# Three tiles of x loaded one by one ahead of the second weights, in a matmul with 2:4-pruned weights

## The chip, the cores and the metric

The kernel runs on one core of a Trainium2 chip. The metric is the device time of one execution in microseconds (us), the median of several runs. A profiled execution gives the trace: when every instruction of every engine started and ended, when every transfer was issued and when it landed.

TensorE (PE) multiplies, and loads its stationary operand beside that (PEld). VectorE (DVE), ScalarE (ACT) and GpSimd (POOL) work elementwise. SyncE (SP) and ScalarE issue the transfers (DMAs).

## The reference

```
x: (16, 512, 1024) bf16    w: (1024, 1024) bf16    b: (1024) bf16

wg   = w.reshape(256, 4, 1024)            # groups of 4 rows, for each column
mag  = abs(wg)
thr  = the second largest of each group's 4 magnitudes
mask = (mag >= thr)
wp   = (wg * mask).reshape(1024, 1024)
out  = einsum("bsd,df->bsf", x, wp) + b
```

So of every four weights that follow each other along the input dimension, the two largest in magnitude stay; the product is that of 8192 tokens with the pruned weights.

## The kernel before

**Tiles.** The 8192 tokens are 64 tiles of 128. The input dimension (1024) is cut into two halves of 512 (g = 0 and 1), the output dimension into halves or quarters. A tile's full product is 16 matmuls of 128x128 by 128x512: 8 steps along the input for each of two output halves.

**The weights and their pieces.** The first half of the weights (g = 0) comes in four pieces of 256 columns (pieces 0 to 3), the second (g = 1) in two of 512 (pieces 4 and 5). Each is loaded with the four members of a group side by side (`w_sb`, `load_w`), so that VectorE can compare them elementwise: abs; `hi` and `lo`, the larger and the smaller of each pair; `t1`, the smaller of the two `hi`; `t2`, the larger of the two `lo`; `thr`, the larger of `t1` and `t2`; `mask`; `mult`, which writes the pruned weights `wp` (class `Piece`, L155 to L193; L177 is abs, L166 the others). Piece 0's four loads are split by rows between two queues (L124, L125); the loads of piece 1 (L130) are called "the second weights" here.

**The start.** TensorE can use `wp` at once only against x in the same order, with the four members of a group apart. For the first seven tiles (`NPK`) this is made on TensorE: a tile's first 512 inputs are loaded as they lie (`load_x`), transposed by four matmuls against a unit matrix (`transpose`, L197 to L203, into a PSUM buffer of the pool `psum_t`, two buffers, or, for tile 4, of `psum_o`, six buffers) and copied out by ScalarE (`copy_xt`, L207). Then each of these tiles is multiplied with pieces 0 to 3 as soon as they are pruned (`mm_piece`, L236). Two tiles share a PSUM bank (`pairs`), and ScalarE copies a finished bank to SBUF (`stage`, L272).

**After that** all tiles use weights in natural order: `spread` (L153) copies `wp` to `wp_nat` by DMA, and x comes transposed by DMA (`load_lead` L118, `load_low` L244, `load_nat` L416). Matmuls against `wp_nat` are at L250. `closes` finishes the first twelve tiles, a loop goes over the other 52. VectorE adds the bias on the way out (L442, L444), ScalarE's queue stores. The last `LATE` tiles are stored in two halves each, the others in one store.

**The orders.** While the weights are pruned, the order on each engine is written out as a list of tokens (L274 to L296), one list for each engine. A planner, not part of the kernel, made them; `run` (L399) only emits each engine's tokens in that order, once what a token needs has been emitted. The tokens are these:

- `T5a` transposes tile 5, `C5a` copies it out, `F4` is four filler matmuls.
- `M5.0g` multiplies tile 5 with part g of piece 0. Parts: x and y are the first and the last two members of the groups; u, v, one member each; g and h the last two members, columns 0 to 127 and 128 to 255 of the piece.
- `abs1`, `hi1`, ..., `mult1x` are the pruning steps of piece 1; `S3b0` stages a pair's bank, `U6h0` tile 6's.
- `W0.1` spreads weights, `X1` and `Y1` are loads of transposed x, `Z` loads the last weights and the bias, `E0`, `A0h0` start products against `wp_nat`.

An instruction waits where it stands in its engine's list, and all that is behind it waits too. TensorE starts with 20 fillers (L409, L410), which read constants only.

The loads at the start are issued in this order, on SP's queue unless "act" is named:

```
    load_w(0, 0, 256, 0, 2)
    load_w(0, 0, 256, 2, 4, "act")
    load_x(5, 6, "act")
    load_x(SOLO, SOLO + 1, "act")
```

(`SOLO` is tile 6), and then L129 to L136: tiles 3 and 4 in one transfer, the second weights, tile 2, tiles 0 and 1, the weights of pieces 2, 3 and 4, and the transposed load of tiles 7 to 11.

Of the kernel before, what the change touches and what calls it, by code (L numbers as in the profile page):

```python
# [10 lines left out]
def kernel(  # L11
# [8 lines left out]
    P = 128  # L20
    bf16 = mybir.dt.bfloat16
    fp32 = mybir.dt.float32
# [10 lines left out]
    FH = 512  # L33
# [8 lines left out]
    STG = 8  # L42
    SOLO = 6
    GROUPS = ((0, 3), (3, 6), (6, 7))
    LATE = 6
    sizes = (4, 8, 8, 8, 8, 8, 8)
    batches = []
    t0 = NPK + LEAD
# [11 lines left out]
    psum_t = ctx.enter_context(tc.tile_pool(name="psum_t", bufs=2, space=bass.MemoryType.PSUM))  # L60
    psum_o = ctx.enter_context(tc.tile_pool(name="psum_o", bufs=6, space=bass.MemoryType.PSUM))
# [38 lines left out]
    def issue(eng, out_, in_):  # L100
        q = nc.sync if eng == "sp" else nc.scalar
        return seq(eng, q.dma_start(out_, in_))  # L102
# [4 lines left out]
    def load_x(ta, tb, eng="sp"):  # L107
        xs = const.tile([P, tb - ta, HK], bf16, name=f"x_{ta}")
        xv, n = tokens(xf, ta)
        issue(eng, xs[:], xv[:, n:n + tb - ta, :HK])  # L110
        for t in range(ta, tb):
            x_sb[t] = xs[:, t - ta, :]
# [13 lines left out]
    load_x(5, 6, "act")  # L126
    load_x(SOLO, SOLO + 1, "act")
    act(nc.scalar.activation(spark[:], nc.const_aps.tensor(1.0, [P, 1], bf16), Act.Abs))
    load_x(3, 5)  # L129
    load_w(0, 256, 512)  # L130
    load_x(2, 3)
    load_x(0, 2)
    load_w(0, 512, 768)
    load_w(0, 768, 1024)
# [58 lines left out]
                self.tt(wp[:, self.g, ms, self.c0 + ca:self.c0 + cb], self.w[:, ms, ca:cb], self.mag[:, ms, ca:cb], Alu.mult)  # L193

    xpk = {}

    def transpose(t):  # L197
        xg = x_sb[t].rearrange("p (q m) -> p m q", m=4)
        bank = psum_o.tile([P, FH], fp32, name="ps") if t == 4 else psum_t.tile([P, FH], fp32, name="tp")
        tp = bank[:].bitcast(bf16)[:, :FH].rearrange("p (m q) -> p m q", m=4)  # L200
        for m in range(4):
            pe(nc.tensor.transpose(tp[:, m, :], xg[:, m, :], ident[:]))  # L202
        xpk[t] = tp  # L203
# [4 lines left out]
        xpk[t] = xt  # L208

    ps_open = {}  # L210
    SPLIT = {0: 6}
    part = {"": slice(0, 4), "x": slice(0, 2), "y": slice(2, 4), "a": slice(0, 2), "b": slice(2, 4)}
    part.update({c: slice(m, m + 1) for m, c in enumerate("uvst")})
    part.update({c: slice(2, 4) for c in "gh"})
    cols = {"g": (0, 128), "h": (128, 256), "j": (0, 128), "k": (128, 256)}
    half = {"a": slice(0, 1), "b": slice(1, 2)}
    pairs = [(3, 4), (SOLO, NPK), (0, 1), (2, 5)]
    pair_of = {t: q for q, pr in enumerate(pairs) for t in pr}
# [48 lines left out]
    def stage(key):  # L267
        solo = key[1] == "h"
        q, h, at = (pair_of[key[0]], key[2], int(key[0] != SOLO)) if solo else (key[0], key[1] // 2, key[1] % 2)
        if (q, h) not in staged:  # L270
# [2 lines left out]

    order = {  # L274
# [7 lines left out]
        ),  # L282
        "dve": (
# [4 lines left out]
        ),  # L288
        "act": (
            "C5a C3a C4a C6a C2a C0a C1a S3b0 S2b0 abs3 S0b0 U6h0 S3b1 S0b1 S2b1 S3b2 S0b2 S2b2 S2b3 S0b3 U6h1 "  # L290
            "S3b3 U7h0 W1.0q U7h1"
        ),
        "sp": (
            "W0.0 Z W0.1 X1 W1.0p Y1 W1.1 Y0"
# [1 line left out]
    }  # L296
    written = {"X0"}
    p = {}
    halves = {0: tuple("ghuv"), 1: ('x', 'y'), 2: ('u', 'v', 'y'), 3: ('x', 'y')}

    by_rows = {0}

# [1 line left out]
        return [tok + x for x in halves.get(i, ("",))]  # L304

    def split_tok(tok):
        k = tok[-1] if tok[-1] in "xyabuvstghjk" else ""
        return (tok[:-1] if k else tok), k

    transposed = []  # L310

    def needs(eng, tok):
        base, k = split_tok(tok)
        if tok[0] == "C":
            return ["T" + tok[1:]]
        if tok[0] == "T":
            return ["C" + transposed[-2]] if tok != "T4a" and len(transposed) > 1 else []
        if tok[0] == "F":
            return []
        if tok[0] == "W":  # L320
            g, h = map(int, tok[1:4].split("."))
            return [n for i, pc in enumerate(pieces) if pc[0] == g and pc[1] // FH == h for n in all_of(f"mult{i}", i)]
        if tok[0] in "XYZ":
            return ["A0h1"] if tok == "Y1" else []
        if tok[0] == "A":
            return ["X0", f"W0.{tok.split('h')[1]}"] + ([f"U{NPK}h{tok[-1]}"] if tok[1] == "3" else [])
        if tok[0] == "E":
            return ["X0", f"W0.{tok[1]}"]
        if tok[0] == "U":
            t, h = map(int, tok[1:].split("h"))  # L330
            if t == NPK:
                return [f"E{h}"]
            return [f"M{t}.{x}" for i, pc in enumerate(pieces) if pc[0] == 0 and pc[1] // FH == h for x in all_of(str(i), i)]
        if base[0] == "M":
            t, i = base[1:].split(".")
            return [f"C{t}a", f"mult{i}{k}"]
        if tok[0] == "S":
            q, n = map(int, tok[1:].split("b"))
            return [f"M{t}.{x}" for i, pc in enumerate(pieces) if pc[0] == 0 and pc[1] // CW == n
                    for t in pairs[q] for x in all_of(str(i), i)]  # L340
        i, step = base[-1], base[:-1]
        before = {"abs": [], "hi": ["abs"], "lo": ["abs"], "t1": ["hi"], "t2": ["lo"],
                  "thr": ["t1", "t2"], "mask": ["thr", "hi", "lo"], "mult": ["mask"]}[step]
        out_ = []
        for b_ in before:
            if b_ in ("t1", "thr") and int(i) in SPLIT:
                out_ += [b_ + i + s for s in {"j": "j", "k": "k", "g": "j", "h": "k"}.get(k, "jk")]
            elif b_ == "t2":
                out_.append(b_ + i)
            elif b_ in ("abs", "hi", "lo") and int(i) in by_rows:  # L350
                out_ += [b_ + i + k] if step in ("hi", "lo") else [b_ + i + s for s in "ab"]
            else:
                out_.append(b_ + i + (k if b_ == "mask" else ""))
        return out_

    def emit(eng, tok):
        base, k = split_tok(tok)
        if tok[0] == "T":
            transpose(int(tok[1:-1]))
            if tok != "T4a":  # L360
                transposed.append(tok[1:])
        elif tok[0] == "F":
            filler(int(tok[1:]))
        elif tok[0] == "W":
            g, h = map(int, tok[1:4].split("."))
            spread(g, h * FH, (h + 1) * FH, {"": range(4), "p": range(2), "q": range(2, 4)}[tok[4:]], eng)
        elif tok[0] == "Z":
            load_w(1, 512, 1024)
            sp(nc.sync.dma_start(bias_sb[:], b.partition_broadcast(P)))
        elif tok[0] == "X":  # L370
            xnat.update(load_lead(int(tok[1:])))
        elif tok[0] == "Y":
            xnat.update(load_low(int(tok[1:])))
            if tok == "Y1":
                tc.add_manual_dep(tails["sp"].ins, ends["A0h1"].ins.name, SYNC, reason="let the spread of the lower weights pass")
        elif tok[0] == "E":
            open_solo(int(tok[1:]))
        elif tok[0] == "U":
            t, h = map(int, tok[1:].split("h"))
            stage((t, "h", h))  # L380
        elif tok[0] == "A":
            open_nat(*map(int, tok[1:].split("h")))
            ends[tok] = tails["pe"]
        elif tok[0] == "C":
            copy_xt(int(tok[1:-1]))
        elif tok[0] == "M":
            mm_piece(*map(int, base[1:].split(".")), part[k], cols.get(k))
        elif tok[0] == "S":
            stage(tuple(map(int, tok[1:].split("b"))))
        else:  # L390
            i = int(base[-1])
            if i not in p:
                p[i] = Piece(i)
            if eng == "act":
                p[i].abs_act()
            else:
                p[i].do(base[:-1], part.get(k, slice(0, 4)), half.get(k, slice(0, 2)), cols.get(k))
# [82 lines left out]
    for bi, (tb, nb) in enumerate(batches):  # L480
        if bi:
            load_batch(bi + 1)
        for j in range(nb):
            t = tb + j
            xt = xnat[t]
            o = outp.tile([P, Dout], bf16, name="o")
            if t == NT - 1:
                for n, (c0, c1) in enumerate(((0, FH), (FH, FH + CW), (FH + CW, Dout - P), (Dout - P, Dout))):
                    ps = psum_o.tile([P, FH], fp32, name="ps")
# [44 lines left out]
```

## Time and profile before

| | |
|---|---|
| Median of 3 runs | 232.64 us (232.62 to 232.73) |
| The profiled execution | 232.79 us |
| Its span, first instruction to last | 231.0 us |
| VectorE busy | 107.8 us, 47% |
| ScalarE busy | 13.3 us, 6% |
| Matmuls against `wp_nat` (L250, x from `xb`) | 831, 178.9 us busy, 375 ns each |
| Products of the first seven tiles (L236) | 126, 12.9 us busy, 261 ns each |
| Transposes (L202, into `tp`) | 24, 2.1 us busy, 220 ns each |
| Transfers, mean over the span | 165 GB/s |

The profile counts an engine as busy from an instruction's start to its modelled end. Matmuls are pipelined: one starts well before the one in front of it has ended, so the distance from start to start is what an instruction costs, and the mean time of one is longer. The chain of work that ended last is followed back from the last instruction: at each step to what released it, or to the instruction before it on its engine. In rows in order of time the first number is the start, the second the length, both in us, and x is the count; "L250" is a line of the kernel. "Idle before" is an engine's idle time and what ended it. For a transfer the last number is the time from issue to landing.

### The profile page before, as it was taken

To read this page: it belongs to the slowest core of one execution; us is meant where nothing else is said; L and a number is where in the kernel's file an instruction comes from. 1 tells how busy PE (TensorE), PEld (TensorE's weight loads), DVE (VectorE), ACT (ScalarE), POOL (GpSimd) and SP (SyncE) were. 2 spreads that over 40 slices of the span, in tenths; PEclk is the share of its full clock that TensorE was granted. 3 is DMA by queue.
4 is the path that set the end of the run, shared out by engine and by line. 5 is a ranking of instruction groups with operands and counts; after the bars stand their busy time and mean duration, and the time that the engine had idled before them with its cause. 6 is when DMAs were issued, how large, how long until landed. Compare 5 with 4: busy or idle time off the path is not lost.

```text
span 231.0 us, 2846 instructions
## 1 busy us (share of the span) xinstructions
PE 226.1 (98%) x1142; PEld 110.9 (48%) x1162; DVE 107.8 (47%) x196; ACT 13.3 (6%) x26; POOL 17.6 (8%) x15
## 2 busy tenths in 40 slices
PE   7999999999999999999999999999999999999995
PEld 4985444444444444444444444444444444444443
DVE  3999787844424424424424424423423423433434
ACT  3665100000000000000000000000000000000000
POOL 1000199700000000000000000000000000000000
PEclk9999999999999999999999999999999999999999
DMA  6999799997399222991159821796129952122122
GB/s 210 296 216 238 190 208 224 290 282 266 134 239 272 82 91 72 229 287 69 72 125 236 229 94 71 144 255 197 63 91 198 219 176 84 53 91 91 54 85 91
DMA packets 79292, 38.19 MB, mean 165 GB/s; under 512 B 64176, under 2 KB 71728, under 8 KB 79280
## 3 DMA queue, kind: packets, MB, share of 16 engines
q1 hardware_dynamic: 68352, 20.75, 44.2%
q10 hardware_dynamic: 10928, 17.27, 21.3%
q8 instruction: 9, 0.15, 0.3%
q14 instruction: 3, 0.02, 0.0%
HBM read 3.28 MB, written 16.78 MB: 87 GB/s over the span
## 4 chain that ended last, share of the span: by engine, by line
PE 96%; DMA 2%; issue 1%; ACTq 0%; DVE 0%
PE ps L250 88%; PE ps L236 5%; PE tp L250 2%; DMA x<-in_x_dram 2%; PE tp L202 1%; ACTq L102 0%; DVE o L442 0%; PE ps L145 0%; PE ps L202 0%
## 5 line engine op out<-in xcount | busy, mean ns | idle before, releaser
L250 PE MATMUL ps<-wp_nat,xb 128*128 128x512 bf16 (+1 forms) x831 | 178.9, 375 | 0.9
L250 PEld LDWEIGHTS <-xb 128*128 128x128 bf16 x848 | 82.4, 98 | 97.5
L442 DVE TENSOR_TENSOR o<-ps,bias_sb 128x512 bf16<-128x512 f32 (+1 forms) x112 | 71.6, 677 | 113.7 <-PE ps L250 111.4
L438 POOL TENSOR_TENSOR st<-st,bias_sb 128x1024 f32<-128x1024 f32 x8 | 16.7, 2122 | 0.0
L250 PE MATMUL ps<-wp_nat,xlead 128*128 128x512 bf16 x63 | 14.7, 379 | 0.1
L250 PEld LDWEIGHTS <-xlead 128*128 128x128 bf16 x88 | 8.6, 98 | 10.2
L236 PE MATMUL ps<-wp,xt 128*128 128x256 bf16 (+1 forms) x126 | 12.9, 261 | 0.0
L444 DVE TENSOR_TENSOR o<-ps,st 128x512 bf16<-128x512 f32 x16 | 11.1, 692 | 2.8 <-PE ps L250 2.2
L236 PEld LDWEIGHTS <-xt 128*128 128x128 bf16 x126 | 11.2, 98 | 1.2
L250 PE MATMUL ps<-wp_nat,xlow 128*128 128x512 bf16 x47 | 10.6, 379 | 0.1
L272 ACT COPY st<-ps 128x512 f32<-128x512 f32 x14 | 7.4, 594 | 3.0 <-PE ps L236 3.0
L250 PEld LDWEIGHTS <-xlow 128*128 128x128 bf16 x48 | 5.0, 103 | 5.4
L166 DVE TENSOR_TENSOR wp<-w_sb,mag 128x256 bf16<-128x256 bf16 (+2 forms) x13 | 6.2, 483 | 0.1
L166 DVE TENSOR_TENSOR mag<-mag,hi 128x256 bf16<-128x256 bf16 (+2 forms) x13 | 6.0, 484 | 0.1
L250 PE MATMUL tp<-wp_nat,xlead 128*128 128x512 bf16 x23 | 5.8, 379 | 0.0
L145 PE MATMUL ps<-const-bfloat16-1.0 128*128 128x128 bf16 (+1 forms) x24 | 4.2, 345 | 0.8 <-PEq L518 0.8
L177 DVE TENSOR_SCALAR mag<-w_sb 128x512 uint16<-128x512 uint16 (+2 forms) x6 | 2.7, 467 | 3.6 <-DMA w_sb<-in_w_dram 3.6
L145 PEld LDWEIGHTS <-const-bfloat16-1.0 128*128 128x128 bf16 x24 | 2.3, 124 | 2.4 <-issue 2.4
L166 DVE TENSOR_TENSOR hi<-mag 128x512 bf16<-128x512 bf16 (+2 forms) x7 | 3.2, 459 | 0.0
L166 DVE TENSOR_TENSOR lo<-mag 128x512 bf16<-128x512 bf16 (+2 forms) x7 | 3.1, 458 | 0.0
L202 PE MATMUL tp<-ident,x 128*128 128x128 bf16 x24 | 2.1, 220 | 0.4 <-DMA x<-in_x_dram 0.4
L207 ACT COPY xt<-tp 128x256 f32<-128x256 f32 x6 | 2.1, 374 | 2.6 <-PE tp L202 2.6
(18 smaller groups left out, 15.0 us busy)
## 6 DMA issues: line engine op xcount, KB each, us to landing
out_dram<-o ACTq DMA_DIRECT2D x58, 256.0 KB, 2.5
wp_nat<-wp SPq DMA_DIRECT2D x14, 128.0 KB, 3.3
out_dram<-o ACTq DMA_DIRECT2D x10, 128.0 KB, 1.7
w_sb<-in_w_dram SPq DMA_DIRECT2D x2, 512.0 KB, 4.6
w_sb<-in_w_dram SPq DMA_DIRECT2D x3, 256.0 KB, 4.6
x<-in_x_dram SPq DMA_DIRECT2D x2, 256.0 KB, 4.0
x<-in_x_dram ACTq DMA_DIRECT2D x2, 128.0 KB, 3.6
bias_sb<-in_b_dram SPq DMA_DIRECT2D x1, 256.0 KB, 4.7
```

The lines of the kernel that those rows point to most:

```text
L145: pe(nc.tensor.matmul(warm_ps[:, :rep * P], lhsT=nc.const_aps.tensor(1.0, [P, P], bf16), rhs=nc.const_aps.tensor(1.0, [P, rep * P], bf16), ...
L166: dve(nc.vector.tensor_tensor(out, a, b_, op=op))
L177: dve(nc.vector.tensor_single_scalar(self.mag[:, ms, :].bitcast(u16), self.w[:, ms, :].bitcast(u16), 0x7FFF, op=Alu.bitwise_and))
L202: pe(nc.tensor.transpose(tp[:, m, :], xg[:, m, :], ident[:]))
L207: act(nc.scalar.copy(xt[:].bitcast(fp32), xpk[t].bitcast(fp32)))
L236: pe(nc.tensor.matmul(ps[:, c0 + ca + d:c0 + cb + d], lhsT=xpk[t][:, m, :], rhs=wp[:, g, m, c0 + ca:c0 + cb], start=(new and m == ms.start ...
L250: pe(nc.tensor.matmul(ps, lhsT=xt[:, kt - koff, :], rhs=wp_nat[:, kt, c0:c1], start=(kt == first), stop=(kt == last)))
L272: act(nc.scalar.copy(staged[(q, h)][:, at, :, :].rearrange("p t c -> p (t c)"), ps_open.pop(key)[:]))
L438: pool(nc.gpsimd.tensor_tensor(st[:], st[:], bias.to_broadcast([P, 2, 2, CW]), op=Alu.add))
L442: dve(nc.vector.tensor_tensor(o[:, c0:c1], ps, bias_sb[:, c0:c1], op=Alu.add))
L444: dve(nc.vector.tensor_tensor(o[:, c0:c1].rearrange("p (n c) -> p n c", n=2), ps.rearrange("p (n c) -> p n c", n=2), add, op=Alu.add))
```

## The change

Tiles 3 and 4, one transfer before, become two, and tile 2's transfer moves ahead of the second weights. All four order lists are made anew. Tile 2's transpose stands ahead of the first product. Tile 6's transpose uses a `psum_o` buffer, as tile 4's did (`LOOSE`), and no longer waits for the copy of an earlier transpose. Piece 0's parts u and v (one member, 256 columns) become e and f (the first two members, 128 columns each), so its products go from six for each tile to eight (`SPLIT`); piece 2's parts become x and y. The abs of piece 2 moves from VectorE to ScalarE. `LATE` goes from 6 to 5, so tile 58 is stored in one transfer. The abs of piece 5 is emitted only after its load has been (`Z`).

```diff
-    LATE = 6
+    LATE = 5
...
-    load_x(3, 5)
+    load_x(3, 4)
+    load_x(4, 5)
+    load_x(2, 3)
     load_w(0, 256, 512)
-    load_x(2, 3)
     load_x(0, 2)
...
+    LOOSE = (4, 6)
...
-        bank = psum_o.tile([P, FH], fp32, name="ps") if t == 4 else psum_t.tile([P, FH], fp32, name="tp")
+        bank = psum_o.tile([P, FH], fp32, name="ps") if t in LOOSE else psum_t.tile([P, FH], fp32, name="tp")
...
-    SPLIT = {0: 6}
+    SPLIT = {0: 8}
...
+    part.update({c: slice(0, 2) for c in "ef"})
-    cols = {"g": (0, 128), "h": (128, 256), "j": (0, 128), "k": (128, 256)}
+    cols = {"e": (0, 128), "f": (128, 256), "g": (0, 128), "h": (128, 256), "j": (0, 128), "k": (128, 256)}
...
         "pe": (
-            "T5a T3a T4a F4 T6a M5.0g M3.0g M5.0h M3.0h M4.0g M4.0h T2a M6.0h M3.0u M6.0u M5.0u T0a M4.0u T1a "
-            "M2.0h M2.0g M2.0u M6.0g M0.0u M0.0h M0.0g M1.0g M0.0v M2.0v M1.0v M5.0v M6.0v M3.0v M4.0v M1.0u "
-            "M1.0h M2.1y M3.1y M5.1y M2.1x M6.1y M0.1x M1.1x M4.1x M6.1x M5.1x M0.1y M4.1y M3.1x M1.1y M2.2y "
...
+            "T5a T3a T4a F4 T6a T2a M5.0h M3.0h M5.0g M4.0g M3.0g M4.0h M6.0g M4.0f M3.0f M2.0f M6.0h M6.0f M2.0g "
+            "T0a T1a M5.0f M6.0e M5.0e M3.0e M4.0e M0.0f M0.0e M2.0e M0.0h M1.0e M0.0g M2.0h M1.0g M1.0f M1.0h "
+            "M6.1x M1.1x M0.1x M3.1x M5.1x M6.1y M4.1y M0.1y M3.1y M4.1x M5.1y M2.1x M1.1y M2.1y M2.2y M5.2y "
...
         "dve": (
-            "abs0a abs0b hi0a lo0a lo0b hi0b t20 t10j t10k thr0j thr0k mask0g mask0h mult0g mult0h mask0u abs1 "
-            "mult0u hi1 lo1 t11 t21 mask0v thr1 mult0v mask1y mask1x mult1y abs2 mult1x lo2 hi2 t22 t12 thr2 "
-            "mask2y mask2v mult2y mask2u mult2v hi3 lo3 t13 t23 mult2u thr3 mask3x mult3x mask3y mult3y abs4 hi4 "
...
+            "abs0a abs0b lo0a hi0b lo0b hi0a t20 t10k t10j thr0k thr0j mask0h mask0g mult0h mult0g mask0f mask0e "
+            "mult0f abs1 mult0e lo1 hi1 t21 t11 thr1 mask1x mult1x mask1y hi2 mult1y lo2 t12 t22 thr2 mask2y "
+            "mult2y lo3 mask2x hi3 mult2x t13 t23 thr3 mask3x mult3x mask3y mult3y abs4 hi4 lo4 t24 t14 thr4 "
...
         "act": (
-            "C5a C3a C4a C6a C2a C0a C1a S3b0 S2b0 abs3 S0b0 U6h0 S3b1 S0b1 S2b1 S3b2 S0b2 S2b2 S2b3 S0b3 U6h1 "
+            "C5a C3a C4a C6a C2a C0a C1a abs2 S3b0 S0b0 S2b0 abs3 U6h0 S2b1 S3b1 S0b1 S0b2 S3b2 S2b2 U6h1 S0b3 "
...
-    halves = {0: tuple("ghuv"), 1: ('x', 'y'), 2: ('u', 'v', 'y'), 3: ('x', 'y')}
+    halves = {0: tuple("efgh"), 1: ('x', 'y'), 2: ('x', 'y'), 3: ('x', 'y')}
...
-            return ["C" + transposed[-2]] if tok != "T4a" and len(transposed) > 1 else []
+            return ["C" + transposed[-2]] if int(tok[1:-1]) not in LOOSE and len(transposed) > 1 else []
...
-        before = {"abs": [], "hi": ["abs"], "lo": ["abs"], "t1": ["hi"], "t2": ["lo"],
+        before = {"abs": ["Z"] if i == "5" else [], "hi": ["abs"], "lo": ["abs"], "t1": ["hi"], "t2": ["lo"],
```

SP's list of tokens is the same in both.

More of the change, by code (lines that the diff above doesn't have):

```diff
@@ L275 @@
         "pe": (
[6 rows of a table removed]
[6 rows of a table added]
         ),
         "dve": (
[4 rows of a table removed]
[4 rows of a table added]
         ),
         "act": (
-            "C5a C3a C4a C6a C2a C0a C1a S3b0 S2b0 abs3 S0b0 U6h0 S3b1 S0b1 S2b1 S3b2 S0b2 S2b2 S2b3 S0b3 U6h1 "
-            "S3b3 U7h0 W1.0q U7h1"
+            "C5a C3a C4a C6a C2a C0a C1a abs2 S3b0 S0b0 S2b0 abs3 U6h0 S2b1 S3b1 S0b1 S0b2 S3b2 S2b2 U6h1 S0b3 "
+            "S2b3 S3b3 U7h0 W1.0q U7h1"
         ),
@@ L306, in split_tok @@
     def split_tok(tok):
-        k = tok[-1] if tok[-1] in "xyabuvstghjk" else ""
+        k = tok[-1] if tok[-1] in "xyabuvstefghjk" else ""
         return (tok[:-1] if k else tok), k
@@ L345, in needs @@
         for b_ in before:
-            if b_ in ("t1", "thr") and int(i) in SPLIT:
-                out_ += [b_ + i + s for s in {"j": "j", "k": "k", "g": "j", "h": "k"}.get(k, "jk")]
+            if b_ == "Z":
+                out_.append(b_)
+            elif b_ in ("t1", "thr") and int(i) in SPLIT:
+                out_ += [b_ + i + s for s in {"j": "j", "k": "k", "e": "j", "f": "k", "g": "j", "h": "k"}.get(k, "jk")]
             elif b_ == "t2":
@@ L359, in emit @@
             transpose(int(tok[1:-1]))
-            if tok != "T4a":
+            if int(tok[1:-1]) not in LOOSE:
                 transposed.append(tok[1:])
```

8 rows, old and new, of the table order are left out of this document.

## The prediction

> **What bounds the kernel now.** I read the page's busy times first, then the chain of work that ended last, then the first 20 us of TensorE, VectorE, ScalarE and the DMA issues in order of time.
>
> ```profile
> PE 226.1 (98%) x1142; PEld 110.9 (48%) x1162; DVE 107.8 (47%) x196; ACT 13.3 (6%) x26; POOL 17.6 (8%) x15
> ...
> PE 96%; DMA 2%; issue 1%; ACTq 0%; DVE 0%
> ```
>
> TensorE is busy 98% of the 231.0 us span and is 96% of the chain. The rest lies at the two ends, so an edit pays only if it takes time out of TensorE's row. The chain, in order of time, around its first product:
>
> ```profile
> 1.26 3.64 DMA x<-in_x_dram
> 4.90 0.05 issue
> 4.95 0.64 PE tp L202 x8
> 5.59 0.22 PE ps L202 x4
> 5.81 0.23 PE ps L145 x4
> 6.04 0.22 PE tp L202 x4
> 6.27 0.03 issue
> 6.29 0.83 PE ps L236 x12
> 7.12 0.22 PE tp L202 x4
> ...
> 8.34 11.04 PE ps L236 x108
> ```
>
> TensorE waits for tile 5 of x until 4.95, transposes tiles 5 and 3 (x8), 4 (L202 into ps), runs four fillers (L145), transposes tile 6, and begins the products at 6.29; from there to 228.37 the chain names TensorE alone. The row 7.12 is tile 2's transpose. The chain looks gapless even before 6.29, but its ends are modelled. TensorE's starts, in order of time, show more:
>
> ```profile
> 5.42 0.39 PE L202 MATMUL ps<-ident,x 128*128 128x128 bf16 x4
> 5.65 0.40 PE L145 MATMUL ps<-const-bfloat16-1.0 128*128 128x128 bf16 x4
> 5.88 0.38 PE L202 MATMUL tp<-ident,x 128*128 128x128 bf16 x4
> 6.29 0.27 PE L236 MATMUL ps<-wp,xt 128*128 128x128 bf16 x2
> ```
>
> Four instructions of 128 columns take (5.65 - 5.42) = 0.23 us start to start, 0.056 each; so the four from 5.88 are through at 6.10, and the array stands until 6.29: **0.19 us** of hidden waiting. VectorE's row says for what:
>
> ```profile
> 5.95 0.49 DVE L166 TENSOR_TENSOR wp<-w_sb,mag 128x256 bf16<-128x256 bf16 x2
> ...
> 11.33 0.29 DVE L166 TENSOR_TENSOR hi<-hi 128x256 bf16<-128x256 bf16 x1
> 11.65 0.29 DVE L166 TENSOR_TENSOR hi<-hi,lo 128x256 bf16<-128x256 bf16 x1
> ...
> 14.86 0.43 DVE L166 TENSOR_TENSOR mag<-mag,hi 128x512 bf16<-128x512 bf16 x1
> 15.31 0.42 DVE L166 TENSOR_TENSOR wp<-w_sb,mag 128x512 bf16<-128x512 bf16 x1
> ```
>
> The first multiply of piece 0 starts at 5.95, takes 0.29, ends at 6.24; the first product starts 0.05 later. The other four rows price a thing used below: an operation that needs the result of the one just before it starts 0.03 after that one's end (11.62 to 11.65, 15.28 to 15.31), while independent ones of 256 elements start every 0.20 and of 512 every 0.34.
>
> **The change, part by part.** *Tile 2's transpose moves ahead of the first product.* It costs four instructions of 0.056 = 0.22, before at 7.12 on the path, now from 6.10 to 6.33. Of it 0.19 fills the hidden wait, so the first product goes from 6.29 to 6.33 and what follows is 0.22 shorter: net **-0.19 us**. It cannot come earlier than 6.29 in any case, since the thirteen VectorE operations before the first multiply are the same in number and size, in another sequence, behind the same two weight loads.
>
> *Whether tile 2 is there.* The issues on SP's queue before, and the time to landing of the second row's first one:
>
> ```profile
> 1.75 0.68 SPq L102 DMA_DIRECT2D w_sb<-in_w_dram  x1
> 2.46 1.08 SPq L102 DMA_DIRECT2D x<-in_x_dram  x2
> ...
> x<-in_x_dram SPq DMA_DIRECT2D x1, 128.0 KB, 4.2
> ```
>
> Tile 2 was issued at 2.46, behind 256 KB of the second weights, and landed 4.2 later, at 6.64. From 2.5 to 9.5 us the trace has 2.32 MB, 331 GB/s, nearly every slice over 90% busy: landing follows bytes. 256 KB are 0.79 us, so without the weights ahead it lands at about 5.85. Its issue, third behind two of 0.46, is at about 2.25; the least time from issue to landing in this queue is 2.8 (first weights), so the bounds are 5.05 and 6.64, and I take 5.85, by bytes. The transpose can use it from 6.10: **0 us**, with 0.2 to spare.
>
> *Splitting tiles 3 and 4* adds an issue of 0.46 on SP and moves no bytes. SP's queue goes: second weights from 1.75 to about 2.75; then tiles 0 and 1 from 3.11 to 3.76, since the ninth load of the kernel waits for the completion semaphore of the first weights (before, that was the third weight load: SP's row stops at 3.54 and goes on at 3.75), and tiles 0 and 1 are now the ninth; behind it in SP's queue stand the third, fourth and fifth weight loads and the transposing load of tiles 7 to 11, each some 0.5 later. By bytes the second weights land where tile 2 did, 6.64, and tiles 0 and 1 at 7.42 as before. If landing followed issue instead they would come at 7.26 and 8.07. Needed: the second weights at 6.96 (below), tiles 0 and 1 at 6.33 + 26 products x 0.056 = 7.78. I take 0, as the stretch is saturated. Further down: the transposing load issues for 5.14 us, so the spreads of the pruned weights that stand behind it go from 10.97 to about 11.4 and the last lands at about 16.8; the first product that reads them is at 19.22: 2.4 us of cover.
>
> The Trainium skill, DMA: Bandwidth & Descriptors, "Rules for kernel authors", speaks against the split: many small transfers are to be coalesced, for each pays a fixed cost, about 2.0 us by its fit. By it, if that cost fell between the two halves, the sum would be some +1 us instead of -0.1 (an estimate from that page). The trace speaks against it: the 256 KB pair landed 3.7 after issue and the 128 KB of tile 2 4.2, with others in flight. It is the last rival below.
>
> *Piece 0 in quarters of columns.* Products per tile go from 4x128 + 2x256 columns to 8x128. From the last row of the chain, with 14 of its 108 at 0.056, the 256-wide take (11.04 - 0.78)/94 = 0.109. So each pair of quarters costs 2x0.056 - 0.109 = 0.002, 14 of them **+0.03 us**. On VectorE 2 masks and 2 multiplies of 256 elements replace 2 and 2.
>
> *VectorE's order, and a new wait.* Before, the first product of piece 1 came at 6.29 + 12x0.056 (transposes of tiles 2, 0, 1) + 28x0.056 + 14x0.109 = 10.05. After, TensorE would be ready at 6.33 + 8x0.056 + 56x0.056 = 9.90. VectorE, in its new order: second multiply 6.15, the two left masks 6.36 and 6.56, third multiply 6.76, abs of piece 1 at 6.96 (needs the second weights), fourth multiply 7.30, lo 7.50, hi 7.84, then 8.17 and 8.37 for the two of 256. Now four operations follow that each need the one before: threshold 8.69, mask 9.01, multiply 9.47 to 9.89. With 0.05 on top the product starts at **9.95**: a wait of 0.05 on TensorE that was not there. Behind it in TensorE's queue stands everything else. So -0.19 + 0.03 + 0.05, or 10.05 to 9.95: **-0.10 us**. All that TensorE does after is the same in number and size.
>
> *Thin margins from there.* The same walk gives for the next halves of pieces 1, 2 and 3 readiness 10.96, 12.93, 14.28, 15.91, 16.70 against TensorE at 11.04, 13.00, 14.31, 16.06, 16.71: no wait, but 0.01 to 0.15 of cover. Bounds: 0 to +0.10.
>
> *abs of piece 2 goes to ScalarE*, 0.34 of VectorE against 1.06 (its row for piece 3), from 8.73 to 9.79, needed at 10.15: 0. Behind it wait the copies of open accumulators; the first is done by 10.33, its bank needed at 10.82. *Tile 6's transpose in the other pool* and *one split store fewer* (tile 58, five tiles of some 3.4 us before the end): 0.
>
> Sum: -0.10 on a span of 231.0. The profiled execution took 232.79, 0.15 above the median of 232.64, and 1.79 around the span, unchanged. On the median: **232.54 us**.
>
> **The rivals.** *Tile 2 late (slower).* Its transpose now stands before all products. It decides from a landing after 6.05; if it lands at 6.64, as it did, the transposes start at 6.69 instead of 6.10, +0.59 - 0.10: 233.13. For it: 6.64 is the only landing this transfer has in the trace. Against: those 256 KB are now behind it. *Second weights or tiles 0 and 1 late.* If landing follows issue, tiles 0 and 1 at 8.07 hold TensorE 0.30 at 7.78, and the abs at 7.31 instead of 6.96 delays piece 1 by 0.35; the two overlap, +0.35 - 0.10: 232.89. Against it, the saturated engines. *The waits eat the gain*, if VectorE's dependent chain runs 0.1 longer: 232.64; for it the thin margins. *More gain:* without any wait 232.46; over 0.47 would need the first weights to land earlier as well, though they lead both queues. *The split itself costs:* the least issue to landing is 2.8, less 0.39 for 128 KB at 331 GB/s is 2.4 that isn't transfer; if tile 4 paid it after tile 3's landing (4.96) it would come at 7.4, its transpose at 7.4 instead of 5.42, the first product at 7.4 + 16x0.056 = 8.3, that of piece 1 at 11.9 instead of 10.05: 234.5. Against it, three loads issued within 0.5 us landed within 0.5 us (4.90, 4.96, 5.44).
>
> **How the numbers follow.** Forecast 0.60; second weights or tiles 0 and 1 late 0.15; tile 2 late 0.11; gain eaten 0.07; more gain 0.05; split 0.02. A measurement of this kernel tells about 0.2%, 0.47 us, from no change. Slower by more: tile 2 late 0.11, split 0.02 and 0.02 of the late second weights, 0.15. Faster by more: 0.04 of the more gain. Within: the rest, 0.81. The range runs from the gain without waits, less 0.1 of scatter between runs, to a little over the late second weights: 232.35 to 233.0.
>
> **What would show it.** Right: the tile-2 transposes between 6.1 and 6.33, the first product at 6.33 or a little before, tile 2 landed before 6.0, the first piece-1 product near 9.95 with VectorE's multiply ending 0.05 before, TensorE's last product 0.1 earlier. Wrong: a TensorE wait on x at 6.1 or 7.8, an abs of piece 1 that starts after 7.0 behind the weights, or a wait behind VectorE over 0.1 at one of the five margins.

## The result and the profile after

The changed kernel takes 233.3 us (median of 7 runs, 233.09 to 233.98) against 232.7 (232.62 to 232.85): ratio 1.0024, interval 1.0013 to 1.0035. It is slower, by some 0.6 us, where 0.1 us of gain was forecast, and it lies above the range. In three more sets of the same kernel, below, its median lies 0.29 to 0.44 above that of the kernel before; the intervals of two of these three include no change.

The page after, its busy times and its chain by engine:

```profile
PE 226.0 (98%) x1156; PEld 111.0 (48%) x1176; DVE 107.9 (47%) x193; ACT 14.1 (6%) x27; POOL 17.6 (8%) x15
...
PE 96%; DMA 2%; issue 1%; SPq 0%; DVE 0%
```

TensorE's work is the same but for fourteen matmuls more, from the quarters of piece 0; what changed can't be read from shares. The chain of the kernel after, in order of time (start, length, what), can be laid beside that of before:

```profile
1.75 4.39 DMA x<-in_x_dram
6.14 0.05 issue
6.18 0.41 PE ps L204 x4
6.60 0.23 PE ps L146 x4
6.83 0.22 PE ps L204 x4
7.05 0.22 PE tp L204 x4
7.27 1.45 PE ps L239 x26
8.73 0.45 PE tp L204 x8
9.17 10.85 PE ps L239 x114
20.02 0.86 PE tp L253 x4
```

In order: tile 4's transfer, tile 4's transpose (L204 into `ps`), the fillers, tiles 6 and 2, the products. Before, this chain started at a transfer that was in at 4.90 and VectorE's multiply set the first product. Now tile 4, issued at 1.75, lands at 6.14, and everything up to the first product stands behind it. The row at 20.02 was at 19.39 in the chain of before:

```profile
19.39 0.86 PE tp L250 x4
```

So the 0.63 us are all lost ahead of it. TensorE's and VectorE's starts in order of time say the same of the kernel after (in brackets the idle time before the row, and what ended it):

```profile
6.18 0.41 PE L204 MATMUL ps<-ident,x 128*128 128x128 bf16 x4 [1.18 <-DMA x<-in_x_dram]
...
7.11 0.39 PE L239 MATMUL ps<-wp,xt 128*128 128x128 bf16 x4
```

```profile
7.31 0.43 DVE L178 TENSOR_SCALAR mag<-w_sb 128x1024 uint16<-128x1024 uint16 x1 [0.41 <-DMA w_sb<-in_w_dram]
...
9.83 0.42 DVE L167 TENSOR_TENSOR wp<-w_sb,mag 128x512 bf16<-128x512 bf16 x1
```

TensorE stood 1.18 us for tile 4. VectorE waited for the second weights (landed 7.28) and began abs of piece 1 at 7.31 rather than 6.96 as forecast, so its multiply ended at 10.25 instead of 9.89. That costs nothing: TensorE, late from tile 4, reaches that product at 7.11 + 64 x 0.056 = 10.69.

The sum is short. First the start of the products against the natural weights, before (L250) and after (L253):

```profile
19.22 1.03 PE L250 MATMUL tp<-wp_nat,xlead 128*128 128x512 bf16 x4
```

```profile
19.86 0.59 PE L253 MATMUL tp<-wp_nat,xlead 128*128 128x512 bf16 x2
```

The first product of all moved from 6.29 to 7.11, +0.82. From there to the first product against the natural weights it takes 12.74 us instead of 12.93, -0.18 (4 x 0.056 for the transpose moved ahead, less 0.04 for the other edits). Together +0.63, from 19.22 to 19.86; the two profiled executions differ by 233.45 - 232.79 = 0.66.

That start, of the first product against the natural weights, is called W below. The time of a profiled execution less its W is 213.57 to 213.77 us in all fourteen traces of this study, so what a kernel here gains or loses is in W, to within 0.2 us.

### The profile page after: what moved, and what is told of

It reads as the page before. It is cut to its first block, busy times and chain, and to the rows that moved or that the text cites. A ratio compares the mean times of both kernels' runs of the same rounds, so it can differ in the third digit from the quotient of the medians.

```text
span 231.7 us, 2872 instructions
## 1 busy us (share of the span) xinstructions
PE 226.0 (98%) x1156; PEld 111.0 (48%) x1176; DVE 107.9 (47%) x193; ACT 14.1 (6%) x27; POOL 17.6 (8%) x15
## 4 chain that ended last, share of the span: by engine, by line
PE 96%; DMA 2%; issue 1%; SPq 0%; DVE 0%
PE ps L253 88%; PE ps L239 5%; PE tp L253 2%; DMA x<-in_x_dram 2%; SPq L102 0%; PE tp L204 0%; PE ps L204 0%; DVE o L447 0%; PE ps L146 0%
## 5 line engine op out<-in xcount | busy, mean ns | idle before, releaser
L253 PE MATMUL ps<-wp_nat,xb 128*128 128x512 bf16 (+1 forms) x831 | 178.9, 375 | 0.9
L253 PEld LDWEIGHTS <-xb 128*128 128x128 bf16 x848 | 82.4, 98 | 97.6
L253 PE MATMUL ps<-wp_nat,xlead 128*128 128x512 bf16 x63 | 14.7, 379 | 0.1
L253 PEld LDWEIGHTS <-xlead 128*128 128x128 bf16 x88 | 8.6, 98 | 10.2
L253 PE MATMUL ps<-wp_nat,xlow 128*128 128x512 bf16 x47 | 10.6, 379 | 0.1
L253 PEld LDWEIGHTS <-xlow 128*128 128x128 bf16 x48 | 5.0, 103 | 5.4
L167 DVE TENSOR_TENSOR wp<-w_sb,mag 128x512 bf16<-128x512 bf16 (+2 forms) x12 | 6.1, 512 | 0.2
L167 DVE TENSOR_TENSOR mag<-mag,hi 128x512 bf16<-128x512 bf16 (+2 forms) x12 | 6.0, 511 | 0.2
L253 PE MATMUL tp<-wp_nat,xlead 128*128 128x512 bf16 x23 | 5.8, 379 | 0.0
L204 PEld LDWEIGHTS <-x 128*128 128x128 bf16 x28 | 1.7, 114 | 1.4 <-DMA x<-in_x_dram 1.3
```

The source lines that it names most:

```text
L167: dve(nc.vector.tensor_tensor(out, a, b_, op=op))
L253: pe(nc.tensor.matmul(ps, lhsT=xt[:, kt - koff, :], rhs=wp_nat[:, kt, c0:c1], start=(kt == first), stop=(kt == last)))
```

## The experiments

A transfer is recorded in sixteen parts, and it has landed when the last of them is in. One traced execution for each row; times in us:

| trace | tiles 3 / 4 | tile 6 | tile 2 | second weights | tiles 0, 1 | first product | W |
|---|---|---|---|---|---|---|---|
| before | 4.96 together | 5.44 | 6.64 | 6.26 | 7.42 | 6.29 | 19.22 |
| before, 2nd trace | 4.91 | 5.84 | 7.02 | 6.68 | 7.81 | 6.27 | 19.48 |
| before, 3rd | 4.94 | 5.88 | 7.04 | 6.67 | 7.83 | 6.17 | 19.50 |
| after | 3.98 / 6.14 | 6.31 | 6.50 | 7.28 | 8.06 | 7.11 | 19.86 |
| after, 2nd | 4.33 / 5.81 | 6.01 | 6.29 | 7.12 | 7.86 | 6.78 | 19.53 |
| after, 3rd | 3.98 / 5.72 | 5.92 | 6.16 | 6.95 | 7.67 | 6.69 | 19.44 |
| after, 4th | 3.98 / 5.64 | 6.10 | 6.33 | 7.06 | 7.80 | 6.63 | 19.37 |
| after, 3 and 4 together | 5.00 | 6.39 | 6.19 | 7.18 | 7.95 | 6.92 | 19.66 |
| before, 3 and 4 split | 3.92 / 5.80 | 6.00 | 7.13 | 6.62 | 8.08 | 6.56 | 19.75 |
| before, tile 2 ahead | 4.83 | 6.05 | 5.83 | 6.79 | 7.58 | 6.35 | 19.42 |
| after, transposes later | 3.96 / 5.76 | 5.97 | 6.20 | 6.98 | 7.98 | 6.10 | 19.75 |
| after with before's loads | 4.83 | 5.46 | 6.62 | 6.25 | 7.41 | 6.36 | 19.63 |
| the same, tile 2's product later | 5.07 | 5.34 | 6.80 | 6.26 | 7.62 | 6.59 | 19.55 |
| tiles 3, 4, 5 in one | 6.63 | 4.10 | 6.51 | 7.65 | 8.42 | 7.83 | 20.58 |

**One part alone, and one undone.** Four kernels on one chip: the changed one with tiles 3 and 4 in one transfer again; the one before with only the split; the one before with only tile 2's load moved; the changed one once more.

```diff
# e1_pair, on the changed kernel
-    load_x(3, 4)
-    load_x(4, 5)
+    load_x(3, 5)
# e2_split, on the kernel before
-    load_x(3, 5)
+    load_x(3, 4)
+    load_x(4, 5)
# e3_move, on the kernel before
-    load_w(0, 256, 512)
     load_x(2, 3)
+    load_w(0, 256, 512)
```

> The changed kernel, with tiles 3 and 4 of x in one transfer again; tile 2 still ahead of the second weights, all orders as changed. Split theory (tile 4's own transfer lands late, and TensorE stands before its transpose): tile 4 lands before 5.1 with tile 3, no wait of TensorE on x after its first transpose, first product at 6.15 to 6.35, time 232.4 to 232.6. Move theory (three x loads ahead of the second weights crowd the start): a wait of TensorE on x of 0.5 us or more stays, time 233.0 or more.

> The kernel before, with nothing changed but that tiles 3 and 4 are two transfers; tile 2 stays behind the second weights, orders as before. Split theory: tile 4 lands after 5.9, its transpose starts then instead of at 5.4, the first product at 6.6 or later, time 233.0 to 233.4. Move theory: tile 4 lands by 5.2, time 232.6 to 232.8.

> The kernel before, with nothing changed but that tile 2 is loaded ahead of the second weights; tiles 3 and 4 in one transfer, orders as before. Split theory: tile 2 lands near 5.85, the second weights near 6.64, no new wait of TensorE over 0.1 us, time 232.6 to 232.8. Move theory: x lands late, time 233.0 or more.

> The changed kernel once more, for a second trace. If tile 4's lateness comes with the split, it lands after 5.9 again and TensorE waits about 1 us before its transpose, time 233.0 to 233.6. If the first trace was an accident of one execution, tile 4 lands before 5.4 and the time is 232.4 to 232.7.

Against the kernel before in the same comparison (233.14): pair 233.37, 1.0009 (0.9997 to 1.0022); split 233.77, 1.0019 (1.0006 to 1.0031); move 233.49, 1.0008 (0.9994 to 1.0023); the changed kernel 233.43, 1.0005 (0.9991 to 1.0018). By time alone only the split is clearly slower. The pair misses its expected gain, and the split and the move came out slower than the 233.0 to 233.4 and the 232.6 to 232.8 expected. Tile 4 was late again with the split, in both its traces, at 5.80 and 5.81, a little less than the 5.9 expected. The traces say more. The chain of the kernel with the split alone:

```profile
3.58 4.50 DMA x<-in_x_dram
8.08 0.05 issue
8.12 0.41 PE tp L203 x4
```

This is a second wait, some 0.23 us for tiles 0 and 1, whose issue the split moved from 3.11 to 3.58; tile 4 had already come at 5.80 and made the first product 6.56. With the pair back in the changed kernel, tile 4 is there at 5.00, and the chain starts elsewhere:

```profile
1.79 4.61 DMA x<-in_x_dram
6.39 0.05 issue
6.44 0.41 PE ps L203 x4
6.86 0.22 PE tp L203 x4
7.08 1.45 PE ps L238 x26
```

Issued at 1.79 is tile 6, on ScalarE's queue. It landed at 6.39 and holds the products until 6.92. So undoing the split removes one wait and uncovers another, for a transfer that the change doesn't touch. Had tile 6 come on time too, tile 2 (6.19) was next.

The move alone isn't free either. Its chain:

```profile
1.79 4.27 DMA x<-in_x_dram
6.05 0.05 issue
6.10 0.41 PE tp L202 x4
```

This is tile 6 again. It landed at 6.05, where the forecast had left it at 5.44, and TensorE stood 0.23 us for it; VectorE stood 0.35 us for the second weights (6.79). Expected was no new wait over 0.1. W is 19.42, 0.20 above the first trace of before and a little under its other two.

Why does the split make tile 4 late, though it moves no bytes? Each engine's busy time, DMA share and GB/s from 3.5 to 4.0 us: before, after, the split alone, and the pair in the changed kernel.

```profile
3.50:4.00 0.50, 0.50 (x8) 0.50 (x7) 0.41 (x3) 0.26 (x2) 0.00 (x0) 1.00 1.09 385
```

```profile
3.50:4.00 0.50, 0.50 (x9) 0.50 (x8) 0.50 (x3) 0.26 (x2) 0.00 (x0) 1.00 0.84 281
```

```profile
3.50:4.00 0.50, 0.50 (x7) 0.50 (x6) 0.50 (x4) 0.27 (x2) 0.00 (x0) 1.00 0.91 283
```

```profile
3.50:4.00 0.50, 0.50 (x7) 0.50 (x6) 0.50 (x3) 0.26 (x2) 0.00 (x0) 1.00 1.04 356
```

The last two columns matter: 385 and 356 GB/s with the pair, 281 and 283 with the split; over all kernels with the pair 350 to 385, with the split 217 to 309. In the records of single packets, SP's queue after the change sends tile 3's last packet at 3.45 and tile 4's first at 3.66, 1.9 us after its issue at 1.75. With 256 KB in that slot packets run on until 4.29, and the next load's begin at 4.17. So in this trace the queue ran dry between two small loads.

That explains only a small part. What was not moved in this half microsecond is (385 - 281) x 0.5 us = 52 KB, some 0.16 us at the 331 GB/s of the prediction (an estimate). In two other traces with the split (after, 2nd and 3rd) tile 4's first packet follows tile 3's last within 0.01 us, and tile 4 landed at 5.81 and 5.72 all the same. From 4.0 to 4.5 us the two groups overlap: 239 to 328 GB/s with the pair, 236 to 311 with the split.

What sets the landing is the last of the sixteen parts. By 5.1 us the pair had landed in all seven traces, and of tile 4's parts nine to thirteen were in; the last came at 5.64 to 6.14. Such late parts aren't the split's own. In the kernel before, the first and the last part of tile 6 and of the second weights, both third on their queues, are 0.53 and 0.65 us apart in the first trace, 0.91 and 1.10 in the second, 1.03 and 1.12 in the third. The split moves tile 4 from the second place to the third. That tile 4 comes late by the split is shown; why parts come late in that place is not, and whether the dry queue has a share in it is not shown either.

**The transposes later.** If the price is only that the transposes of late tiles stand ahead of the products, moving them behind eight products should take it away.

```diff
-            "T5a T3a T4a F4 T6a T2a M5.0h M3.0h M5.0g M4.0g M3.0g M4.0h M6.0g ...
+            "T5a T3a F4 M5.0h M3.0h M5.0g M3.0g T4a T6a T2a M4.0g M4.0h M6.0g ...
...
+    loose = {t: psum_o.tile([P, FH], fp32, name="ps") for t in LOOSE}
-        bank = psum_o.tile([P, FH], fp32, name="ps") if t in LOOSE else psum_t.tile([P, FH], fp32, name="tp")
+        bank = loose[t] if t in LOOSE else psum_t.tile([P, FH], fp32, name="tp")
```

Beside it ran the kernel before and the changed kernel, neither with an edit.

> The changed kernel with the transposes of tiles 4, 6 and 2 moved on TensorE from ahead of the first product to behind the first eight products (tiles 5 and 3, whose x is there early); loads and the other orders as changed. If the late x in front of the products is the loss: no TensorE wait on x over 0.15 us behind the first transposes, first product at 6.1 to 6.35, piece 1 begins when VectorE has it (second weights landing + 2.95, near 10.2), 0.2 to 0.5 us less than the changed kernel. If the loss is elsewhere: the same time as the changed kernel within 0.1 us.

> The kernel before, once more, for a second trace of it. Theory of scatter (from the third transfer of each queue on, one or two of the sixteen parts of every load come about 1 us late in some executions, whatever the kernel): its tile 6 and its second weights, the loads issued near 1.75, have parts spread over 0.8 us or more. Theory of the split (only many single-tile loads cause it): all spreads stay at 0.65 us or less, as in the first trace.

> The changed kernel, timed beside the two that follow, on the same chip: tile 4 after 5.5, TensorE waits on it 0.5 to 1.3 us, ratio to before 1.001 to 1.003.

Before against itself: 0.9999 (0.9988 to 1.001). The changed kernel: 233.28 against 232.91, 1.0012 (1.0002 to 1.0022), as expected, with tile 4 at 5.72. The second trace of before answers what its expectation asks: late parts come there too (0.91 and 1.10 us from first to last), so many single-tile loads aren't needed for them. The late transposes: 233.58, 1.0034 (1.0022 to 1.0045), slower where a gain was expected. TensorE's starts in that kernel:

```profile
6.10 0.61 PE L240 MATMUL ps<-wp,xt 128*128 128x128 bf16 x8 [0.77 <-DVE wp L167]
6.54 0.61 PE L205 MATMUL ps<-ident,x 128*128 128x128 bf16 x8
6.99 0.39 PE L205 MATMUL tp<-ident,x 128*128 128x128 bf16 x4
7.40 1.23 PE L240 MATMUL ps<-wp,xt 128*128 128x128 bf16 x18
```

The wait for x is gone and the first product is at 6.10, where VectorE allows it. But TensorE now idles 0.77 for VectorE, and the twelve transposes, 12 x 0.056 = 0.67, stand behind the first product; 0.19 of waiting for a copy comes on top (6.99 + 4 x 0.056 = 7.21, and the next product is at 7.40). W is 19.75. Transposes ahead of the first product are nearly free until about 6.15, because VectorE isn't ready earlier, so delaying them gives that time away.

**The rest without the loads.** The changed kernel's orders and halves, with the loads of before and tile 2's transpose where tile 2 can have landed.

```diff
-    load_x(3, 4)
-    load_x(4, 5)
-    load_x(2, 3)
+    load_x(3, 5)
     load_w(0, 256, 512)
+    load_x(2, 3)
...
-            "T5a T3a T4a F4 T6a T2a M5.0h M3.0h M5.0g M4.0g M3.0g M4.0h M6.0g ...
+            "T5a T3a T4a F4 T6a M5.0h M3.0h M5.0g M4.0g M3.0g M4.0h T2a M6.0g ...
```

> The changed orders on the loads of before: tiles 3 and 4 in one transfer, second weights ahead of tile 2, and tile 2's transpose behind the first twelve products; the other orders as changed. It prices the rest of the change: quarters of piece 0, VectorE's order, abs of piece 2 on ScalarE, one split store fewer. Theory: the rest costs 0 to 0.1 us, ratio to before 0.9995 to 1.0007. Rival: the rest costs more than 0.2 us, by a wait of TensorE behind VectorE or behind a copy of ScalarE.

It took 233.13, 1.0016 (1.0007 to 1.0025). The chain shows that my own edit had made a wait:

```profile
7.43 0.02 issue
7.45 0.38 ACT xt L208
7.83 0.05 issue
7.88 0.62 PE ps L238 x8
```

A product of tile 2 stood ahead of its copy by ScalarE. With that product some places further back:

```diff
-            "... T2a M6.0g M4.0f M3.0f M2.0f M6.0h M6.0f M2.0g T0a T1a M5.0f M6.0e ...
+            "... T2a M6.0g M4.0f M3.0f M6.0h M6.0f M5.0f M2.0f M2.0g T0a T1a M6.0e ...
```

> The changed orders on the loads of before, tile 2's transpose behind twelve products, and now tile 2's own products three places later, so that they don't wait for ScalarE's copy. Theory: the rest of the change costs 0 to 0.1 us: no TensorE wait over 0.1 us between the first product and the first one against natural weights unless a load is late, ratio to before 0.9995 to 1.0007. Rival: the rest costs 0.2 us or more.

233.06 against 232.93, 1.0002 (0.9986 to 1.0018). From the first product to W it takes 12.97 against 12.93 of before: the other edits cost 0.04, where +0.03 was predicted. What the changed kernel loses comes from its loads and from the transposes that wait for them. This version doesn't beat the kernel before; its first product came late, at 6.59, because TensorE's clock rose late in this execution (shown at the end).

**Bytes or place in the queue.** To see whether a load in the second place of its queue comes in time whatever it carries, tiles 3, 4 and 5 went in one transfer (tile 2 then rides on ScalarE's queue, behind tile 6).

```diff
-    load_x(5, 6, "act")
     load_x(SOLO, SOLO + 1, "act")
+    load_x(2, 3, "act")
...
-    load_x(3, 4)
-    load_x(4, 5)
-    load_x(2, 3)
+    load_x(3, 6)
```

Tile 6's transpose and copy go first in both order lists.

> The changed orders with other waves of loads: the first load of SP's queue behind the weights brings tiles 3, 4 and 5 at once, ScalarE's queue tile 6 and then tile 2, the second weights come next on SP. TensorE transposes tile 6 first, then 5, 3, 4, four fillers, 2, all ahead of the products; the rest as changed. If it is the third load of a queue that comes late: tiles 3 to 6 land by 5.4, tile 2 at 5.8 to 6.1, first product at 6.3 to 6.6, the first product against natural weights at 19.1 to 19.4, time 0.999 to 1.001 of before. If the late x comes with any x in front of the second weights: tile 2 or 4 after 6.1 and the ratio at 1.0015 or more.

> The kernel before, a third trace: tiles 3, 4 and 5 by 5.0, tile 6 between 5.4 and 5.9, the last part of a load issued at 1.75 or later 0.5 to 1.1 us behind its first part; first product at 6.25 to 6.35 by either theory.

> The changed kernel, a fourth trace, timed beside the others: first product at tile 4's landing + 0.05 + 16 x 0.056 = landing + 0.95 to 0.97, first product against natural weights 12.74 after it. Tile 4 lands at 5.6 to 6.2, ratio to before 1.001 to 1.003.

The triple took 234.45 against 232.93, 1.0071 (1.0044 to 1.0098); before against itself 0.999 (0.9971 to 1.0009); the changed kernel 233.37, 1.0013 (0.9997 to 1.0029). The triple's chain and its transfer (KB, then issue to landing):

```profile
1.24 5.39 DMA x<-in_x_dram
6.63 0.05 issue
6.68 0.64 PE tp L202 x8
```

```profile
x<-in_x_dram SPq DMA_DIRECT2D x1, 384.0 KB, 5.4
```

384 KB in the second place land at 6.63, later than 128 KB in the third. Twelve of its sixteen parts were in by 5.22, so late parts come in the second place too, and place alone doesn't decide: the theory that only third loads are late fell. Of the three sizes tried there, 256 KB served best. The third trace of before kept its landings as expected, but its first product came at 6.17, earlier than the 6.25 to 6.35 expected by either theory. The fourth of the changed kernel came as expected, with tile 4 at 5.64 and the first product 0.99 behind it.

## Why the prediction failed

**The step that failed** is "landing follows bytes", and with it the price of the split: "adds an issue of 0.46 on SP and moves no bytes ... I take 0, as the stretch is saturated". Tile 4 was not even given a landing of its own. It landed at 5.64 to 6.14 in all six traces with the split and at 4.83 to 5.07 in the seven with the pair. The first product then comes 0.97 to 0.99 later (0.05 of issue, 16 instructions of 0.056, the first one's start-up) in the four traces of the changed kernel, at 6.63 to 7.11 instead of 6.33. From there W is 12.74 later in each. So the loss begins where tile 4 lands after 6.48 - 0.98 = 5.5: W is then that of the first trace of before.

The same step put tile 2 at 5.85 and took tile 6 to land as before, at 5.44. In the four traces of the changed kernel they landed at 6.16 to 6.50 and 5.92 to 6.31. With tile 4 in time they would still have held the first product to 6.46 to 6.83 (an estimate: in the pair kernel it comes 0.52 after tile 6's landing, and from tile 2's landing it would take 0.05 of issue and 0.25 for four instructions, as tile 6's took there). So of the 0.30 to 0.78 that the first product lost against 6.33, the split accounts for 0 to 0.28, and tiles 6 and 2 for the rest. This is why putting the pair back gave almost nothing, 233.37 against 233.43.

The ground for the zero, "331 GB/s, nearly every slice over 90% busy", was a mean over 7 us. It says nothing of half a microsecond at 281 GB/s, and nothing of the last part of a load, which came up to 1.46 us after its first.

**The rival with the right place** was "the split itself costs", at 0.02. It priced a fixed cost after tile 3's landing and came to a first product of 8.3; measured 7.11. The evidence set against it ("three loads issued within 0.5 us landed within 0.5 us") held the answer: tile 6 was a load of 128 KB, third on its queue behind another of 128 KB, the place that the split gives to tile 4 on the other queue, and it landed at 5.44, 0.54 after the one ahead of it, and at 5.84 and 5.88 in the later traces of before. The rule cited from the Trainium skill (DMA: Bandwidth & Descriptors, "Rules for kernel authors", small transfers to be coalesced) pointed the right way, though what it calls mostly overhead is under 64 KB, and 384 KB in one transfer did worse than 256. The fixed cost of 2.0 us named with it is fitted there to transfers issued from GpSimd, and the prediction shows no working for the +1 us made from it. The split alone moved W by 0.53 from the first trace of before and by 0.25 to 0.27 from its others.

**Tile 2 by 5.85:** 6.16 to 6.50. This is the rival "tile 2 late", and it stayed hidden: tile 4's wait ends at 6.14 and tile 2's transpose is third behind it. In the pair kernel it landed at 6.19, just after 6.10, when it was needed. Only the move alone gave the forecast, 5.83, and there tile 6 was late.

**Second weights 6.64, tiles 0 and 1 at 7.42:** 7.28 and 8.06, and 6.95 to 7.12 and 7.67 to 7.86 in the other traces of the changed kernel. The rival by which landing follows issue had said 7.26 and 8.07. It cost nothing only because TensorE was late itself. The wait of 0.05 on VectorE at piece 1's first product therefore never appeared. "It cannot come earlier than 6.29 in any case" was wrong as well, without effect on the result: with the same work on VectorE the first product came at 6.17 in the third trace of before and at 6.10 with the transposes later, where the first weights on ScalarE's queue landed at 3.60 and 3.57 instead of 3.74.

**Right:** tile 2's transpose ahead of the products takes 0.22 out behind them; quarters and orders +0.03, measured 0.04; no wait at any of the thin margins (12.74 from the first product to W, as the sum without waits gives); the later issues on SP, abs of piece 2 on ScalarE, tile 6's other pool and the store of tile 58, all 0, for nothing after W changed (213.6 us in both).

**Not settled:** in the later sets the kernel before has W 19.48 and 19.50, because it then pays waits of its own for tile 2 (0.13 and 0.24) and tiles 0 and 1 (0.10 each). A single trace of the one kernel can thus lie under one of the other (19.37, 19.44); that the changed kernel is slower rests on the medians, 0.60, 0.29, 0.37 and 0.44 us in four sets, of which two have an interval clear of no change. Why the last parts of a load come late stays open, and with it why tile 6 comes later when a tile of x stands third on the other queue.

## What to carry to other kernels

Cutting a load in two isn't free because it moves no bytes: the second half gets a later place in its queue, and a load is in only when its last part is. Look for a load of the same size in the same place, not at the mean rate over the stretch. Before an instruction is moved ahead of a wait that hides it, take the latest landing that its load and every load beside it show in several traces; one trace gives one draw. And undoing a bad part may only uncover the next wait, so read the chain of the undone kernel before giving it the credit.

## What the runs showed of the hardware

The time from issue to landing of 128 KB went from 2.6 us (first weights) to 4.6 (tile 6) within one kernel, with place and company. Two views of the transfers of the pair kernel, by time of issue (queue, KB, issue to landing); first tiles 3 and 4 on SP's queue and tile 5 on ScalarE's, then tile 6 behind it:

```profile
x<-in_x_dram SPq DMA_DIRECT2D x1, 256.0 KB, 3.8
...
x<-in_x_dram ACTq DMA_DIRECT2D x1, 128.0 KB, 3.6
```

```profile
x<-in_x_dram ACTq DMA_DIRECT2D x1, 128.0 KB, 4.6
```

Twice the bytes, on the other queue, took 0.2 longer, one place further back on the queue 1.0. On one queue and in one place, second on SP's, size tells more: 128 KB took 2.7 to 3.1 us (six traces), 256 KB 3.6 to 3.8 (seven), 384 KB 5.4 (one). Tile 6's landing sorts by what stands third on the other queue: 5.34 to 5.88 in the five traces with the second weights there, 5.92 to 6.39 in the eight with a tile of x. The two groups are only 0.04 apart, and the reason wasn't looked for.

Single parts lag. In loads in the second place of their queue the last of the sixteen parts came at most 0.73 us after the first (1.75 for the one of 384 KB), in the third place 0.44 to 1.64, by another amount in each execution: in the first trace after the change thirteen of tile 4's were in by 4.98, the last at 6.14. This sets the landing, and its cause stays open.

The Trainium skill, DMA: Bandwidth & Descriptors, "Latency and other measured facts", gives about 0.6 us to the first byte of a transfer issued from these queues. In the first trace after the change the first load of SP's queue sent its first packet at 1.85, 1.1 us after its issue began and 0.7 after that ended; tile 4's came 1.9 us after its issue began, behind another load.

TensorE's clock doesn't rise at one time. The granted clock is recorded as full from 3.5 to 5.9 us after the start, by execution (twelve of the fourteen traces have that record; in the rows by half microsecond above, 1.00 also stands where there is none yet). Until then instructions of 128 columns start every 0.107 us instead of 0.056. In the second kernel with before's loads it rose at 5.86, and its first transposes took half as long again (0.64 before):

```profile
5.11 0.97 PE tp L203 x8
```

The Trainium skill, TensorE: Matmul & The Clock Gate, "Part 1: The HAM clock gate", gives the same two rates (107 and 56 ns) and a transition that varies by 500 ns to either side, from a window that doesn't start with the kernel; here it varied by 2.4 us.
